# Respacing a weight load, a third band slot for the first group, and another place for table loads in a kernel's own planner

## The chip, the cores and the metric

The kernel runs on one core of one Trainium2 chip. The metric is the device time of one execution in microseconds (us); the figure for a kernel is the median of several runs.

## The reference

Two branches share the input x (2048 rows of 1024, bf16), and a gate mixes them:

```
g = sigmoid((x * gate_w).sum(-1))
a = A(x, wqkv, wo)        # attention over 8 keys at distance 0, 2, ... 14; 32 heads of 32
z = gelu(x @ w_in)        # 2048 x 3584; z1 is the first half, z2 = layernorm(second half)
b = (z1 * (w_sp @ z2 + b_sp)) @ w_out
out = g * a + (1 - g) * b
```

In A, q, k and v come from x @ wqkv. Each position has a softmax over its 8 scores per head, weights the 8 values with it, and the result is multiplied by wo.

## The kernel before, in words

The work is one long sequence of matmuls on TensorE with everything else laid beside it. In order: transposes of x and the v tiles of three head groups (`vp_tile`, L297); the projections q and k of eight groups of four heads (`qk_tile`, matmul L292, copy L295 on ScalarE); v of the other groups by a Strassen scheme (`v_quad`); the z2 half of x @ w_in (`z2_tile` with matmul L821, then `z2_quad`); the z1 half (`z1_quad`); the spatial product; the output product. All Strassen matmuls are recorded at L434.

**Bands.** The scores of a group are small matmuls of q against a band of k (L354), copied from PSUM by ScalarE (L362) into a band slot in SBUF, stored to memory (`band_d`), and loaded back as `att_L` with one row of 8 scores per position (`load_bands`, L649). A band slot can be written again only when its store has been read out. Group 0 has four such copies (`first_bands`): the first into a slot of its own, three into `band_slots`; groups 1 to 7 have three, of which two go into `band_slots`.

**Attention.** VectorE takes maxima of `att_L` (L670 to L673), ScalarE the exponential (L661), VectorE the sums, weights and att_A (L682 to L691), then the products with v (L707) and their sums (L711, L712, L716). The result is stored to `o_d`.

**Gate.** A column of each v tile (copied to `gl_s`, L305, behind the tile's copy L304) holds the gate's sum; one matmul, L404, turns it, once all sixteen are there.

**Weights for z2.** `load_wz(0)` (L800) loads the first half of them in eight parts of two DMAs each. `load_later` (L924) gives the parts to the planner, due at a start and then at equal gaps. Once all eight have landed, four VectorE steps of `wz_sums` (L576) are put in line. The z2 tiles read the weights, the z2 quads the sums too. A later call, `load_later(1, ...)` (L968), does the same for the second half.

**The planner.** From L942 on the order of every engine's instructions is set by a model that runs while the program is written. It has a clock for each of TensorE, ScalarE, VectorE, SP and the DMA engines; `take` (L233) adds a duration to a clock, not sooner than a ready time. Main work (matmuls) is written in a fixed order. Before each step `advance(t)` (L763) picks, by the clocks, which attention steps of VectorE, exponentials of ScalarE and DMAs of SP are written next. The engines then run their instructions in just that order, whatever the true times are. All these DMAs are issued by SP, one after the other. Parts of `load_wz` are "timed": each is made to wait for the last ScalarE instruction that was written before it (L271 to L277), so that it can't start early. The band loads are written only when no band store is still due (L737). A change of ScalarE's function table is counted by `table(name)` (L242).

**The z2 quads.** `chain` (L498) runs seven products. The third, Y, is added to a stored share by VectorE (`plus`, L505), and a later product writes Y again; two quads run in turns, so TensorE has three other products before it needs that sum.

Of the kernel before, what the change touches and what calls it, by code (L numbers as in the profile page):

```python
# [43 lines left out]
R_OFF = XS_OFF + 16384  # L44
# [3 lines left out]
VP = GP * C  # L48
# [5 lines left out]
def _sub_ap(t, offset_elems, dims):  # L54
    return bass.AP(tensor=t.tensor, offset=t.offset + offset_elems, ap=[list(t.ap[0])] + [list(d) for d in dims])
# [3 lines left out]
def kernel(  # L59
# [26 lines left out]
    def reg(off, n):  # L86
        return arena[:, off:off + n]
# [44 lines left out]
    band_slots = [reg(R_OFF + o, 7 * BR).bitcast(F16).rearrange("p (m k h) -> p m k h", m=7, h=HG) for o in (30208, 32196, 38848)]  # L132
    band0 = reg(R_OFF + 34184, 2 * BR).bitcast(F16).rearrange("p (m k h) -> p m k h", m=2, h=HG)
    nc.gpsimd.memset(band0[:, :, 0:W - 1, :], NEG)
    vst_slots = [reg(R_OFF + o, 2 * VR).rearrange("p (a c) -> p a c", a=2) for o in (19968, 34752, 36288, 37824)]
    vp_slots = [reg(R_OFF + o, 4 * VP).rearrange("p (i c) -> p i c", i=4) for o in (36288, 37824, 4096, 5632)]
    vq_slots = [reg(R_OFF + 39360 + 2 * VH * r, 2 * VH).bitcast(F32) for r in range(2)]
    vz_slots = [reg(R_OFF + 19968 + 2 * ZC * r, 2 * ZC).bitcast(F32) for r in range(2)]

# [63 lines left out]
    clock = dict(PE=0.0, ACT=0.0, DVE=0.0, SP=0.0, DMA=0.0)  # L203
# [29 lines left out]
    def take(engine, dur, ready=0.0):  # L233
        clock[engine] = max(clock[engine], ready) + dur
        return clock[engine]

    def pe(dur, ready=0.0):
        return take("PE", dur, ready)

    tables = ["exp"]  # L240

    def table(name):  # L242
        t = 0.0 if tables[0] == name else 1.28
        tables[0] = name
        return t

    def act(dur, ready):
        if live[0]:
            advance(ready)
        return take("ACT", dur, ready)  # L250
# [6 lines left out]
    def dma(ready, dur, f, landed=None, timed=False):  # L257
        if not live[0]:
            return f()
        item = [ready, dur, f, landed, timed]  # L260
        due.append(item)
        return item

    def issue(item):
        if item in due:
            due.remove(item)
            ready, dur, f, landed, timed = item
            sp = take("SP", 0.62, max(ready, lanes[-8]))
            end = take("DMA", 1.2 * dur, sp + 0.6) + 1.1
            lanes.append(end)  # L270
            if timed:  # L271
                settle()
                behind, at = pinned[gate_act.ins.engine], len(nc.cur_bb.bb.instructions)
            f()
            if timed:
                for i in nc.cur_bb.bb.instructions[at:]:
                    tc.add_manual_dep(i, behind, SYNC, reason="not sooner")  # L277
            if landed is not None:
                landed(end)
# [48 lines left out]
    band_at = [0]  # L328
# [7 lines left out]
    def band_blocks(g, first, step, n, pairs=None):  # L336
        qt, kt_ = qT_slots[g % 2], kT_slots[g % 2]
        if first == 0:
            st = band0
        else:  # L340
            st = band_slots[band_at[0] % (3 if g else 2)]
            band_at[0] += 1
        for item in stored.get(id(st), ()):
            issue(item)
        ready = pe(T_BAND * (0.3 if n < 3 else 1.0), band_free[0])
        lo = W - 1 if first == 0 else 0
        for m in range(n):
            e, b = divmod(first + m * step, 8) if pairs is None else (m // pairs, first + m % pairs)
            for q in range(2):
                skip = lo if q == 0 else 0  # L350
                at = P * b + QB * q
                for h in range(HG):
                    hp = slice(DH * h, DH * (h + 1))
                    nc.tensor.matmul(banks[4 + h][QB * q:QB * (q + 1), m * KW + skip:(m + 1) * KW], qt[hp, e, at:at + QB],  # L354
                                     kt_[hp, e, at - (W - 1) + skip:at + QB], start=True, stop=True,
                                     tile_position=(DH * h, QB * q), skip_group_check=True)
        band_free[0] = act(0.55 if n < 3 else 1.73, ready + 0.2) + 0.15
        if lo:
            nc.scalar.copy(st[QB:P, 0:n, 0:lo, :], _sub_ap(psum_all[QB:P, :], 4 * 512, [[KW, n], [1, lo], [512, HG]]))
        dst = st[:, 0:n, lo:KW, :]  # L360
        src = _sub_ap(psum_all, 4 * 512 + lo, [[KW, n], [1, KW - lo], [512, HG]])
        nc.scalar.copy(dst, src)  # L362
        bd = band_d[g]

        def landed(t):
            band_data[g] = max(band_data[g], t)

        stored[id(st)] = []
        for q in range(2):
            for e in range(1 if pairs is None else 2):  # L370
                k = n if pairs is None else pairs
                dst = bass.AP(tensor=bd.tensor, offset=bd.offset + (2 * first + 16 * e + q) * BS, ap=[[BR, QB], [2 * step * BS, k], [1, BR]])
                src = st[QB * q:QB * (q + 1), e * k:(e + 1) * k].rearrange("p m k h -> p m (k h)")
                stored[id(st)].append(dma(band_free[0], 0.1 * k, lambda dst=dst, src=src: sync.dma_start(dst, src), landed))

    def band_set(g, x):
        band_blocks(g, *BAND_SETS[x])
# [422 lines left out]
    def load_wz(p):  # L800
        def part(k):
            for m in range(2):
                sync.dma_start(wz[p][m][:, k:k + 1], win_v[:, k:k + 1, FH + ZC * (2 * m + p):FH + ZC * (2 * m + p + 1)])
        return [lambda k=k: part(k) for k in range(KT)]


    def wz_sums(p):
        w = wz[p]
        return sums4_steps(wzs[p], w[0][:, 0:4], w[0][:, 4:8], w[1][:, 0:4], w[1][:, 4:8])
# [66 lines left out]
    def group_tiles(g):  # L876
        if g + 1 < NG:
            tiles = [lambda t=t, c=c: qk_tile(g + 1, t, c) for t in range(2) for c in range(4)][not g:]
        else:
            tiles = [lambda a=a, m=m: z2_tile(7, a, m) for m in range(2) for a in range(2)]  # L880
        if g == 0:
            return tiles

        def band(x):
            band_set(g, x)
            if x == 2:
                bands_have[0] = g + 1
        band = [lambda x=x, f=band: f(x) for x in range(3)]
        if g + 1 < NG:
            return [tiles[0], band[0], tiles[1], band[1], tiles[2], tiles[3], band[2]] + tiles[4:]  # L890
        return [tiles[0], band[0], tiles[1], band[1], tiles[2], band[2]] + tiles[3:]

    def with_quads(g, main):
        n = NQ[g]
        if not n:
            return main
        steps = [lambda: mark(banks[5:7], ZC)]
        for _ in range(n):
            q = z2_quad(*quads.pop(0), side=1)
            steps += [lambda q=q: next(q)] * 7  # L900
        rest = main[6:]
        out, done = main[0:6], 0
        for m, t in enumerate(rest):
            out.append(t)
            upto = len(steps) * (m + 1) // len(rest)
            out += steps[done:upto]
            done = upto
        return out
# [4 lines left out]
    def behind_first(n):  # L913
        at = [0]

        def f():
            at[0] += 1
            if at[0] == 1:
                mark(banks[5:7], n)
            step()  # L920
        return f

    def play(items):
        for f in items:  # L924
            f()
            step()

    def load_later(p, at, gap):
        land = [0.0]

        def landed(t):
            land[0] += 1
            if land[0] == KT:
                fill.extend((t + LATE, 1.05, f) for f in wz_sums(p))
        for n, f in enumerate(load_wz(p)):
            dma(at + gap * n, 0.65, f, landed, True)

    def load_wqk_later(g, at):
        dma(at, 2.9, lambda: load_wqk(g, sync.dma_start))
# [13 lines left out]
    for g in range(NG):  # L953
        main = with_quads(g, group_tiles(g))
        if g in (1, 2, 3, 4):
            load_wqk_later(g + 3, clock["PE"])
        hold[0] = g == NG - 1
        play(main[0:8 - (not g)])
        if g == 2:
            for i in range(0, 8, 2):  # L960
                run(v_quad(i), v_quad(i + 1), step=behind_first(VH) if i == 0 else step)
            advance(clock["PE"] + 1.0)
            v_have[0] = NG
            next_v()
            load_later(0, clock["PE"] + 6.0, 3.0)
        play(main[8 - (not g):])

    load_later(1, clock["PE"] + 3.0, 2.0)  # L968
# [1 line left out]
    for n in range(0, len(quads), 2):  # L970
        p, i = quads[n]
        if p == 1 or quads[n + 1][0] == 1:
            t = clock["PE"]
# [398 lines left out]
```

## Time and profile before

| | us |
|---|---|
| median of 6 runs | 671.29 (668.59 to 672.04) |
| profiled execution, its own time | 672.14 |
| its span, first to last instruction | 670.4 |
| TensorE busy in the span | 658.7 |
| VectorE busy | 451.7 |
| ScalarE busy | 293.7 |
| DMA queue of SP, share of 16 engines | 60.3% |

A profile is of one execution. A row of a timeline gives start, duration, engine, source line, operation, output and inputs with their sizes, the count of merged instructions, and in square brackets how long the engine had been idle before it and what released it. A row of waits gives who waited for whom: us in total, times, longest. The granted clock is the share of full speed that TensorE was allowed. The lines that matter are shown in the prediction.

### The profile page before, as it was taken

What the parts mean: (1) busy time and instruction counts of PE and PEld (TensorE: products, weight loads), DVE (VectorE), ACT (ScalarE), POOL (GpSimd) and SP (SyncE); (2) the same over time, 40 slices, a digit from 0 to 9 for tenths busy, and PEclk for the clock granted to TensorE, in tenths of its full rate; (3) what the DMA queues carried; (4) which work ended last, traced back from release to release, by engine and by line L of the source; (5) the groups of instructions that cost most, each with busy time, mean ns of one, the idle gap of its engine ahead of it and who ended that gap; (6) DMA issues with size and microseconds to landing.
All of it is one profiled execution on the core that took longest, in us unless ns stands there. A gap on an engine that the chain in (4) does not pass through costs nothing.

```text
span 670.4 us, 10740 instructions
## 1 busy us (share of the span) xinstructions
PE 658.7 (98%) x4194; PEld 316.9 (47%) x4194; DVE 451.7 (67%) x671; ACT 293.7 (44%) x621; POOL 6.6 (1%) x15
## 2 busy tenths in 40 slices
PE   8989999999998999999999999999999999999998
PEld 4544467444444555444444444444444444444444
DVE  1520799966998999998779676797679953333301
ACT  4444676555686668789745112111122122222221
POOL 1000000000000000001100000000000000000000
PEclk9999999999997999999999999999999999999999
DMA  9988564698585132246993578559755788534100
GB/s 213 184 210 229 112 119 129 155 238 176 128 198 121 62 88 67 64 123 171 256 264 125 137 181 165 123 171 292 114 133 148 151 189 198 120 98 101 40 33 32
DMA packets 229475, 98.16 MB, mean 146 GB/s; under 512 B 177440, under 2 KB 215728, under 8 KB 229424
## 3 DMA queue, kind: packets, MB, share of 16 engines
q1 hardware_dynamic: 229136, 97.27, 60.3%
q8 instruction: 33, 0.54, 0.4%
q10 hardware_dynamic: 288, 0.20, 0.1%
q14 instruction: 18, 0.15, 0.1%
HBM read 45.10 MB, written 36.61 MB: 122 GB/s over the span
## 4 chain that ended last, share of the span: by engine, by line
PE 84%; DVE 6%; DMA 4%; SPq 4%; issue 1%; ACT 1%; DVEq 0%; ACTq 0%
PE psum_all L434 68%; PE psum_all L292 12%; SPq L195 3%; DVE arena L707 2%; PE psum_all L302 2%; DMA band_d<-arena 2%; DVE arena L711 1%; PE psum_all L354 1%; DMA att_L<-band_d 1%; SPq L190 1%; DMA arena<-in_A_x_dram 1%; DMA z_d<-arena 1%; DVE arena L712 1%; DVE arena L716 0%; PE psum_all L490 0%
## 5 line engine op out<-in xcount | busy, mean ns | idle before, releaser
L434 PE MATMUL psum_all<-arena 128*128 128x512 bf16 (+5 forms) x2425 | 498.7, 368 | 3.4 <-DVE psum_all L505 3.3
L434 PEld LDWEIGHTS <-arena 128*128 128x128 f16 (+1 forms) x2425 | 238.0, 98 | 263.0 <-issue 8.2
L292 PE MATMUL psum_all<-arena 128*128 128x512 bf16 x512 | 114.8, 379 | 0.0
L292 PEld LDWEIGHTS <-arena 128*128 128x128 bf16 x512 | 48.5, 98 | 56.2 <-issue 0.2
L707 DVE TENSOR_TENSOR arena<-arena,att_A 128x2048 f16<-128x2048 bf16 (+1 forms) x44 | 73.4, 1705 | 0.3
L295 ACT CAST arena<-psum_all 128x512 bf16<-128x512 f32 x64 | 36.9, 587 | 44.8 <-PE psum_all L292 44.7
L580 DVE TENSOR_TENSOR arena<-arena 128x1024 f16<-128x1024 f16 (+3 forms) x31 | 18.8, 608 | 46.1 <-PE psum_all L434 40.8
L452 ACT COPY psum_all<-psum_all 128x512 f32<-128x512 f32 (+1 forms) x30 | 15.8, 527 | 76.6 <-PE psum_all L434 73.0
L814 ACT ACTIVATE arena<-psum_all 128x448 bf16<-128x448 f32 x64 | 34.2, 545 | 23.1 <-DVE psum_all L505 12.9
L505 DVE TENSOR_TENSOR psum_all<-psum_all,arena 128x448 f32<-128x448 f32 (+1 forms) x58 | 37.1, 660 | 6.7 <-PE psum_all L434 4.3
L1094 ACT ACTIVATE arena<-psum_all 128x512 bf16<-128x512 f32 x56 | 31.1, 602 | 22.2 <-PE psum_all L434 13.1
L582 DVE TENSOR_TENSOR arena<-arena 128x1024 f16<-128x1024 f16 (+3 forms) x31 | 18.6, 607 | 31.6 <-PE psum_all L434 18.6
L711 DVE TENSOR_TENSOR arena<-arena 128x2048 f16<-128x2048 f16 (+1 forms) x22 | 37.2, 1704 | 0.1
L362 ACT CAST arena<-psum_all 128x1988 f16<-128x1988 f32 (+3 forms) x25 | 33.9, 1356 | 6.3 <-DMA band_d<-arena 5.1
L476 ACT COPY psum_all<-psum_all 128x512 f32<-128x512 f32 (+2 forms) x30 | 15.6, 522 | 46.2 <-PE psum_all L434 45.2
L458 ACT COPY arena<-psum_all 128x512 f32<-128x512 f32 (+1 forms) x30 | 16.2, 543 | 37.2 <-PE psum_all L434 33.1
L463 ACT COPY psum_all<-psum_all 128x512 f32<-128x512 f32 (+1 forms) x30 | 15.8, 528 | 36.4 <-PE psum_all L434 35.6
L869 ACT ACTIVATE arena<-arena 128x896 bf16<-128x896 bf16 x32 | 30.5, 961 | 0.0
L581 DVE TENSOR_TENSOR arena<-arena 128x1024 f16<-128x1024 f16 (+3 forms) x31 | 18.4, 607 | 10.4 <-PE psum_all L434 10.3
L1296 DVE TENSOR_TENSOR arena<-psum_all,arena 128x512 bf16<-128x512 f32 x8 | 5.5, 691 | 29.3 <-ACT psum_all L476 29.3
L302 PE MATMUL psum_all<-arena 128*128 128x385 bf16 x128 | 22.6, 327 | 0.0
L576 DVE TENSOR_TENSOR arena<-arena 128x512 f16<-128x512 bf16 (+3 forms) x36 | 19.4, 568 | 4.1 <-DMA arena<-in_B_w_in_dram 2.3
(95 smaller groups left out, 402.1 us busy)
## 6 DMA issues: line engine op xcount, KB each, us to landing
arena<-v_d SPq DMA_DIRECT2D x8, 960.0 KB, 7.6
z_d<-arena SPq DMA_DIRECT2D x14, 512.0 KB, 4.8
arena<-z_d SPq DMA_DIRECT2D x14, 512.0 KB, 4.2
zg_d<-arena SPq DMA_DIRECT2D x56, 128.0 KB, 2.2
arena<-zg_d SPq DMA_DIRECT2D x32, 224.0 KB, 3.2
band_d<-arena SPq DMA_DIRECT2D x28, 248.5 KB, 5.0
arena<-in_A_wqkv_dram SPq DMA_DIRECT2D x16, 256.0 KB, 4.3
o_d<-arena SPq DMA_DIRECT2D x4, 1024.0 KB, 6.7
```

The source lines that it names most:

```text
L195: inst = _orig_dmat(*a, **k)
L292: nc.tensor.matmul(ps[:], w[:, t, kt, :], xT[:, kt, 512 * c:512 * (c + 1)], start=(kt == 0), stop=(kt == KT - 1))
L295: nc.scalar.copy(dst[:, :, 256 * c:256 * (c + 1)], ps[:].rearrange("p (n e) -> p e n", e=2))
L302: nc.tensor.matmul(ps[:, 0:VP + 1], xT[:, kt, i * P:(i + 1) * P], wvp[:, kt, :], start=(kt == 0), stop=(kt == KT - 1))
L362: nc.scalar.copy(dst, src)
L434: nc.tensor.matmul(bank[:, 0:N], lhsT, rhs, start=(start and m == 0), stop=(m == n - 1), skip_group_check=True)
L505: last_add[0] = nc.vector.tensor_tensor(out[:, n], a[:, n], vs, ALU.add)
L707: lambda ws=ws, in0=in0, in1=in1: tt(p5[:, ws], in0[:, ws], in1[:, ws], ALU.mult)), False
L711: lambda a=p3[:, ws], b=p3[:, ws.start + 4:ws.stop + 4]: tt(a, a, b, ALU.add)), not n
L814: nc.scalar.activation(z2[:, i + 8 * a, ZC * c:ZC * (c + 1)], bank[:, 0:ZC], ACT.Gelu_apprx_tanh, accum_out=s1[:, 4 * n + c:4 * n + c + 1])
L869: return nc.scalar.activation(junk, src, ACT.Square, accum_out=(s2, s2h)[x][:, n:n + 1])
L1094: last_gelu[0] = nc.scalar.activation(z1s[:, f, a, :], bank[:], ACT.Gelu_apprx_tanh)
```

## The change

The gap between the parts of the first z2 weights goes from 3 to 6 of the planner's microseconds, and the first is due at 4 instead of 6 (last hunk). Group 0 takes turns over three band slots instead of two; since the third slot overlaps the second of the slots for v tiles (`vp_slots`), that one moves from offset 37824 to 16128, inside the second buffer of `v_slots_t`. `table` no longer returns a duration that the caller adds behind the ready time; it advances ScalarE's clock itself, before the caller's ready time is looked at.

```diff
-    vp_slots = [reg(R_OFF + o, 4 * VP).rearrange("p (i c) -> p i c", i=4) for o in (36288, 37824, 4096, 5632)]
+    vp_slots = [reg(R_OFF + o, 4 * VP).rearrange("p (i c) -> p i c", i=4) for o in (36288, 16128, 4096, 5632)]
...
     def table(name):
-        t = 0.0 if tables[0] == name else 1.28
+        if tables[0] != name:
+            take("ACT", 1.28)
         tables[0] = name
-        return t
+        return 0.0
...
         if first == 0:
             st = band0
         else:
-            st = band_slots[band_at[0] % (3 if g else 2)]
+            st = band_slots[band_at[0] % 3]
             band_at[0] += 1
...
             v_have[0] = NG
             next_v()
-            load_later(0, clock["PE"] + 6.0, 3.0)
+            load_later(0, clock["PE"] + 4.0, 6.0)
         play(main[8 - (not g):])
```

## The prediction

> **What bounds the kernel now.** I read the page's first two parts, then TensorE's waits, then the timeline around each wait.
>
> ```profile
> span 670.4 us, 10740 instructions
> PE 658.7 (98%) x4194; PEld 316.9 (47%) x4194; DVE 451.7 (67%) x671; ACT 293.7 (44%) x621; POOL 6.6 (1%) x15
> PEclk9999999999997999999999999999999999999999
> ```
>
> TensorE is busy for 658.7 of 670.4 us. So a change that adds and removes no matmul can win only TensorE's 11.7 us of idle time, and whatever a lowered clock stretches. One slice of the 40, the 13th (201 to 218 us), shows a lowered clock. TensorE's waits name the idle time that other engines cause:
>
> ```profile
> PE psum_all L434 <- DVE psum_all L505: 3.3, 2, 3.1
> PE psum_all L404 <- ACT gl_s L305: 2.2, 1, 2.2
> ```
>
> Start-up takes 2.4 us of the rest and the tail 2.7; both lie outside the change. These two waits are the ones that it can reach.
>
> The 2.2 us wait, in the timeline of all engines:
>
> ```profile
> 40.66 0.48 ACT L304 CAST arena<-psum_all 128x384 bf16<-128x384 f32 x1 [0.72 <-PE psum_all L302]
> 41.03 0.17 ACT L305 COPY gl_s<-psum_all 128x1 f32<-128x1 f32 x1
> 46.29 1.10 ACT L362 CAST arena<-psum_all 128x1136 f16<-128x1136 f32 x1 [5.09 <-DMA band_d<-arena]
> 48.88 0.38 PE L404 MATMUL psum_all<-ident,gl_s 128*16 128x128 f32 x2 [2.24 <-ACT gl_s L305]
> ```
>
> ScalarE stands for 5.09 us in front of L362, the fourth band copy of group 0: it reuses the first slot, whose store is still in flight. Six short copies (L304, L305) stand behind it, and the gate matmul L404 needs the last.
>
> The 3.1 us wait, by TensorE's windows (columns: stretch, its length, busy time and matmuls, granted clock, DMA share, GB/s) and then the timeline of all engines:
>
> ```profile
> 200.00:202.00 2.00, 0.00 (x0) 1.00 1.22 163
> 202.00:203.00 1.00, 0.05 (x1) 0.50 1.05 280
> 208.00:209.00 1.00, 1.00 (x4) 0.59 0.00 0
> 209.00:210.00 1.00, 1.00 (x8) 1.00 0.62 159
> ```
>
> ```profile
> 197.86 4.49 DVE L707 TENSOR_TENSOR arena<-arena,att_A 128x4096 f16<-128x4096 bf16 x2
> 202.27 0.63 DVE L505 TENSOR_TENSOR psum_all<-psum_all,arena 128x448 f32<-128x448 f32 x1
> 202.95 1.28 PE L434 MATMUL psum_all<-arena 128*128 128x448 f16 x3 [3.08 <-DVE psum_all L505]
> ```
>
> VectorE runs two attention products (L707) ahead of the first sum (L505) of the z2 quads, in the order that the program wrote, and comes to L505 late. TensorE idles 3.08 us and then runs at half clock from 202.95 to about 208.8.
>
> Why is VectorE late? Its own timeline, and SP's:
>
> ```profile
> 153.63 0.29 DVE L670 TENSOR_TENSOR att_m<-att_L 128x256 f16<-128x256 f16 x1 [7.58 <-DMA att_L<-band_d]
> 144.37 2.09 SPq L190 DMA_DIRECT2D arena<-in_B_w_in_dram  x2
> 146.55 0.59 SPq L190 DMA_DIRECT2D band_d<-arena  x1
> 147.19 2.60 SPq L190 DMA_DIRECT2D arena<-in_B_w_in_dram  x2
> 149.84 1.28 SPq L190 DMA_DIRECT2D att_L<-band_d  x2
> ```
>
> It stood 7.58 us for the scores of a group (att_L). SP issues from 126 to 151 us with hardly a gap, and seven of the eight pairs of first z2 weights (arena<-in_B_w_in_dram) stand ahead of that att_L load.
>
> **The change, part by part.**
>
> *Third band slot for group 0.* It removes L362's wait for a DMA and adds no instruction. L362 can then start when ScalarE has done L305 at 41.20, with its matmuls already done at 40.89, so about 5 us earlier. The vp tiles whose copies follow end on TensorE at 44.9; the last gl_s copy would be done by about 45.6 (0.48 + 0.17 behind it). L404 stands behind L292, which ends at 46.64, so the whole 2.24 us go. What is late next: nothing before 46.64. Where the 2.2 us could be given back: the stores of these bands do not come sooner, since SP issues eight band stores back to back from 44.97 to 50.19. The scores of group 0 thus still land at 65.5. The exponential that needs them starts at 69.9 on ScalarE, behind TensorE's work in ScalarE's order; 2.2 us sooner is 67.7, still after L673 ends at 66.8. So the attention moves with TensorE. The vp slot that has to make room moves into the second v buffer, which is loaded only after that slot's stores: bounds 0 and about 1 us, on SP beside busy TensorE; I take 0. Gain: **2.2**.
>
> *Spacing of the z2 weights.* The eight pairs took 0.82, 2.28, 1.33, 1.29, 1.13, 2.09, 2.60 and 0.85 us of SP's timeline, 12.4 us in all, 1.55 each. In the planner's time they were due at 6, 9, ... 27; they become due at 4, 10, ... 46. The att_L load fell between the seventh and the eighth (24 and 27). By 24 the new spacing has issued four (4, 10, 16, 22). Three pairs fewer ahead of it: 3 x 1.55 = 4.6 us sooner. VectorE's other waits of this stretch fall with it: 1.07 us at 136.51, for a store of o_d that stands behind the second pair (2.28), and 1.56 us at 159.30, where the weight sums (L576, four of 1.06) waited for the last pair's data. Together 4.6 + 1.07 + 1.56 = 7.2 us of VectorE's time before 202. To meet TensorE, L505 must come 3.08 us sooner (5.3 if VectorE did not share the 2.2 us above). The planner's own order can spend some of the room: one more L707 of 2.29 us in front of L505. That leaves between 7.2 - 3.08 = 4.1 us of margin and 7.2 - 5.3 - 2.3 = -0.4. I count the wait as gone, with a remainder in the sum below.
>
> What the wait is worth: 3.08 us idle, and 5.9 us at half clock, which cost 2.95: **6.0**. The Trainium skill (TensorE: Matmul & The Clock Gate, Part 1) has the clock fall after an idle window of about 3.4 us. By that rule, read as a threshold, a 3.08 us gap would cost 3.1 only, and the whole sum below be 4.8. The clock row shows 0.50 behind this gap, so I take 6.0. The 2.24 us gap at 46.6 shows no fall (1.00 in that stretch).
>
> What the move costs: five pairs pass the att_L loads of later groups on SP. The last pair is due 19 planner microseconds later, so at about 152.6 + 19 = 172. Landing takes a median 3.9 us (page, DMA issues), so 176, against L821 (z2 tiles, which read these weights) at 184.98 - 2.2 = 182.8: 7 us of cover. The sums move from 159 to about 176 and are wanted at about 194.
>
> *Table loads in the planner.* No instruction is added; the planner lets ScalarE's 1.28 us pass before the data is ready. This agrees with the first gelu's load at 185.78, which starts in the row right behind the copy that ends at 185.77 and is done at 187.06, while its matmuls end at 186.66: 0.4 us of it is in the way, not 1.28. The Trainium skill (ScalarE: Activation LUTs, What ACT_TABLE_LOAD costs) adds 1.38 us of drain to each switch. The row has no such gap; by the rule the gelu would start 1.4 us later than it did, and the planner should count 2.66, which would put L505 later again. I take the row: the planner's TensorE clock falls by some 1 us in group 7, which puts L505 a little sooner in VectorE's order. Worth 0 by itself (bounds: +0.5 and -0.5).
>
> *New lateness after 203.* In the old run the half clock let VectorE catch up: between 203 and 350 its L505 waited on TensorE 18 times for 4.3 us. That cover shrinks. The nearest row for what then happens is at 272 to 277, where four L707 in front of L505 cost TensorE 0.31 us. Bounds: 0 and four such L707 (4 x 1.16 = 4.6 us). I take 0.5.
>
> Sum: 2.2 + 6.0 - 0.5 = **7.7 us**. The profiled execution took 672.14 us; it becomes 664.4. It lies 0.85 above the median of the runs (671.29), so the prediction is **663.6**.
>
> **Rivals.**
>
> *The wait stays in part.* For: VectorE is 90 to 100% busy from 160 to 350, and the planner fills new room with attention work. Against: 7.2 us of freed time. If 1.5 to 3 us of waiting remain, with or without the half clock, or come back between 203 and 350, the gain is 3 to 6: 665 to 668.5.
>
> *The spacing does nothing for TensorE.* If att_L is held by its own stores' landing (SP waits up to 2.5 us for band_d) and not by the queue, only the band slot remains: 671.3 - 2.2 = 669.1.
>
> *Slower: the moved pairs hold SP.* Each pair waits, by construction, for the last ScalarE instruction written before it. From 154 to 178 ScalarE itself stands 3.62, 3.42 and 1.56 us for VectorE (L661). If the pairs inherit these 8.6 us and add their own 5 x 1.55 = 7.8, less the some 7 us in which SP was idle between 153 and 190, the later att_L loads come 9.4 us later. That is more than the 7.2 gained: L505 then comes 2.2 us later than before, TensorE 2.2 sooner, the wait grows by 4.4, and the time is 671.3 - 2.2 + 4.4 = 673.5. It decides once those loads come over 7.2 us later. Against: the pairs are due in step with ScalarE's order, and the exponentials come sooner too.
>
> **How the numbers follow.** Main case 0.62 (662 to 665.2), wait in part 0.20 (to 668.5), band slot alone 0.07 (669.1), slower or level 0.11 (to 675). The range 661.5 to 669.0 leaves out the last and a little below. About 0.3%, 2.0 us, can be told from no change: faster 0.86, same 0.05, slower 0.09.
>
> **What would show it.** Right: no wait of L404; L362 without a DMA wait; granted clock 1.00 from 200 to 210; the wait of L670 for att_L near 150 us down from 7.6 to some 3; TensorE's busy time down by 3 to about 655.7, its idle time by 5. Wrong: L821 waiting for in_B_w_in_dram, an att_L wait after 160 us above 3 us, a new clock fall, or TensorE waiting for L505 between 203 and 280.

## The result, and the profile after

| | before | changed |
|---|---|---|
| median, us | 670.53 (36 runs, 667.52 to 674.14) | 665.45 (17 runs, 664.45 to 670.12) |
| ratio to before, 95% interval | | 0.9934 [0.9918, 0.9951] |
| profiled execution, its own time, us | 672.14 | 670.12 |

The ratio of the means is 0.9934, which is 4.4 us [3.3, 5.5] of 670.5; the two medians differ by 5.1. The forecast was 663.6, a gain of 7.7 us: the direction holds, the size does not, and the rival "the wait stays in part" (665 to 668.5) describes what came. The execution that was profiled is the slowest of the changed kernel's 17, as the one of before had been one of the slow ones, so the two pages must not be subtracted from each other. The page of the changed kernel (all its line numbers past 242 are one higher than before: L506 is L505, L708 is L707):

```profile
span 668.0 us, 10747 instructions
PE 659.0 (99%) x4194; PEld 317.1 (47%) x4194; DVE 452.2 (68%) x671; ACT 294.5 (44%) x621; POOL 6.2 (1%) x15
PEclk9999999999998999999999999999999999999999
```

The lowered clock is still there, in the same slice, the 13th (0.8, before 0.7). TensorE's waits, all that are over 1 us:

```profile
PE psum_all L435 <- DVE psum_all L506: 3.3, 1, 3.3
PE psum_all L318 <- DVE arena L313: 1.2, 1, 1.2
```

The gate matmul (L405) is gone from the list; the first sum (L506) is not. The timeline around the gate:

```profile
41.25 0.17 ACT L306 COPY gl_s<-psum_all 128x1 f32<-128x1 f32 x1
41.30 1.12 ACT L363 CAST arena<-psum_all 128x1136 f16<-128x1136 f32 x1
...
45.54 0.17 ACT L306 COPY gl_s<-psum_all 128x1 f32<-128x1 f32 x1
...
46.79 0.39 PE L405 MATMUL psum_all<-ident,gl_s 128*16 128x128 f32 x2
```

L363 follows the copy before it at once; the last gl_s is done at 45.7 (the prediction said 45.6), and L405 has no bracket. So the band slot did what its working said. The other place, TensorE's windows and then VectorE's and TensorE's rows:

```profile
198.00:200.00 2.00, 0.00 (x0) 0.97 0.98 247
200.00:202.00 2.00, 1.00 (x3) 0.50 0.79 149
206.00:208.00 2.00, 2.00 (x11) 0.82 0.90 239
```

```profile
149.40 0.29 DVE L671 TENSOR_TENSOR att_m<-att_L 128x256 f16<-128x256 f16 x1 [6.47 <-DMA att_L<-band_d]
...
200.32 0.63 DVE L506 TENSOR_TENSOR psum_all<-psum_all,arena 128x448 f32<-128x448 f32 x1
...
201.00 11.28 PE L435 MATMUL psum_all<-arena 128*128 128x448 f16 x44 [3.27 <-DVE psum_all L506]
```

The wait for the scores, which was to fall from 7.58 to about 3, is 6.47; TensorE stands 3.27 us instead of 3.08, and the half clock follows (0.50 until 206). SP's rows show the reason's first half:

```profile
136.06 5.37 SPq L190 DMA_DIRECT2D arena<-in_A_wqkv_dram  x2
141.53 2.37 SPq L190 DMA_DIRECT2D arena<-in_B_w_in_dram  x2
143.95 1.28 SPq L190 DMA_DIRECT2D att_L<-band_d  x2
```

Only four pairs of w_in now stand ahead of att_L, three fewer, as foretold. But the load of q and k weights in front of it holds SP for 5.37 us where before it took 2.50, and from the issue of att_L to VectorE's first use of it there are 5.45 us (143.95 to 149.40), before 3.79 (149.84 to 153.63).

### The profile page after: what moved, and what is told of

It reads as the page before. It is cut to its first block, busy times and chain, and to the rows that moved or that the text cites. A ratio compares the mean times of both kernels' runs of the same rounds, so it can differ in the third digit from the quotient of the medians.

```text
span 668.0 us, 10747 instructions
## 1 busy us (share of the span) xinstructions
PE 659.0 (99%) x4194; PEld 317.1 (47%) x4194; DVE 452.2 (68%) x671; ACT 294.5 (44%) x621; POOL 6.2 (1%) x15
## 4 chain that ended last, share of the span: by engine, by line
PE 88%; DVE 5%; DMA 3%; ACT 1%; issue 1%; SPq 0%; DVEq 0%
PE psum_all L435 73%; PE psum_all L293 11%; PE psum_all L303 3%; DVE arena L708 2%; DMA att_L<-band_d 2%; DMA band_d<-arena 1%; PE psum_all L355 1%; DVE arena L712 1%; DMA arena<-in_A_x_dram 1%; DVE arena L713 1%; ACT arena L815 0%; PE psum_all L491 0%; DVE arena L717 0%; ACT arena L363 0%; DVE arena L577 0%
## 5 line engine op out<-in xcount | busy, mean ns | idle before, releaser
L293 PE MATMUL psum_all<-arena 128*128 128x512 bf16 x512 | 114.8, 379 | 0.0
L293 PEld LDWEIGHTS <-arena 128*128 128x128 bf16 x512 | 48.4, 98 | 56.2 <-issue 0.2
L708 DVE TENSOR_TENSOR arena<-arena,att_A 128x2048 f16<-128x2048 bf16 (+1 forms) x44 | 73.3, 1704 | 0.3
L506 DVE TENSOR_TENSOR psum_all<-psum_all,arena 128x448 f32<-128x448 f32 (+1 forms) x58 | 37.5, 661 | 6.5 <-PE psum_all L435 4.5
L712 DVE TENSOR_TENSOR arena<-arena 128x2048 f16<-128x2048 f16 (+1 forms) x22 | 37.2, 1704 | 0.1
L363 ACT CAST arena<-psum_all 128x1988 f16<-128x1988 f32 (+3 forms) x25 | 33.9, 1356 | 1.2 <-PE psum_all L355 0.4
L671 DVE TENSOR_TENSOR att_m<-att_L 128x256 f16<-128x256 f16 x8 | 2.3, 288 | 29.6 <-DMA att_L<-band_d 29.6
```

Source lines behind the costliest of these rows:

```text
L293: nc.tensor.matmul(ps[:], w[:, t, kt, :], xT[:, kt, 512 * c:512 * (c + 1)], start=(kt == 0), stop=(kt == KT - 1))
L506: last_add[0] = nc.vector.tensor_tensor(out[:, n], a[:, n], vs, ALU.add)
L708: lambda ws=ws, in0=in0, in1=in1: tt(p5[:, ws], in0[:, ws], in1[:, ws], ALU.mult)), False
L712: lambda a=p3[:, ws], b=p3[:, ws.start + 4:ws.stop + 4]: tt(a, a, b, ALU.add)), not n
```

## The experiments

All kernels, each against the kernel before on the same chip (e1 to e4 on one, e5 to e8 on a second, f1 to f4 on a third). "Clock" counts executions by their mean granted TensorE clock: 0.999 or 1.00, or 0.997, or 0.992 to 0.995. In the profiles the first means no fall of the clock, the second one stretch of 3.4 us at half clock (it costs up to 1.7 us), and 0.994 or 0.995 two such stretches (up to 3.4 us); no execution at 0.992 was profiled. "Gate" and "sum" are TensorE's waits in us at the gate and at the first sum in the one profiled execution.

| kernel | median us (runs) | ratio [95%] | clock | gate | sum |
|---|---|---|---|---|---|
| before, on two chips | (60) | 1 | 23 / 28 / 9 | 2.24 | 3.08 |
| changed, first result and e4_all | (23) | | 19 / 3 / 1 | 0 | 3.27, 1.09 |
| e1_slot | 667.68 (8) | 0.9960 [0.9941, 0.9979] | 4 / 4 / 0 | 0 | 2.45 |
| e2_space | 669.99 (12) | 0.9994 [0.9973, 1.0014] | 4 / 6 / 2 | 1.63 | 1.35 |
| e3_table | 671.47 (12) | 1.0009 [0.9988, 1.0031] | 5 / 5 / 2 | 1.67 | 2.89 |
| e4_all | 666.18 (6) | 0.9938 [0.9920, 0.9955] | 5 / 1 / 0 | 0 | 1.09 |
| e5_slot_space | 667.03 (12) | 0.9961 [0.9942, 0.9979] | 6 / 6 / 0 | 0 | 2.72 |
| e6_warm | 671.51 (12) | 1.0041 [1.0016, 1.0066] | 3 / 4 / 5 | 1.54 | 2.07 (of an added matmul) |
| e7_lag | 666.86 (12) | 0.9954 [0.9935, 0.9973] | 12 / 0 / 0 | 0 | 0.24 |
| e8_wz24 | 667.20 (12) | 0.9962 [0.9942, 0.9981] | 8 / 3 / 1 | 0 | 0.81 |
| f1_before_less | 667.91 (12) | 0.9970 [0.9950, 0.9990] | 5 / 7 / 0 | 2.81 | 0 |
| f2_all_less | 665.24 (6) | 0.9927 [0.9902, 0.9952] | 6 / 0 / 0 | 0 | 0.82 |
| f3_before_profile | 671.51 (1) | | 0 / 1 / 0 | 2.91 | 3.12 |
| f4_space_profile | 669.13 (1) | | 0 / 1 / 0 | 2.50 | 1.36 |

**Each part alone.** The change has three parts, so the first question is which of them carries the gain. First the band slot:

```diff
-    vp_slots = [... for o in (36288, 37824, 4096, 5632)]
+    vp_slots = [... for o in (36288, 16128, 4096, 5632)]
...
-            st = band_slots[band_at[0] % (3 if g else 2)]
+            st = band_slots[band_at[0] % 3]
```

> The band slot alone (both of its lines), nothing else. All theories: the gate matmul no longer waits (2.2 us before), so the time falls by 2.2 us, 0.9967 of before, if the later part of the kernel shifts along. Theory A (the attention moves with TensorE): the wait of TensorE for the first sum of the z2 quads stays at about 3.1 us, with the clock at half behind it. Rival: the scores land no sooner in absolute time, so that wait grows by up to 2.2 us and the time stays within 0.1% of before.

It gains 2.7 us [1.4, 4.0]. VectorE's wait for att_L is 8.01 (before 7.58): the attention moved with TensorE, as said. Then the spacing:

```diff
-            load_later(0, clock["PE"] + 6.0, 3.0)
+            load_later(0, clock["PE"] + 4.0, 6.0)
```

> The spacing alone. Theory A (fewer weight loads ahead of the scores on SP): the 7.6 us wait of VectorE for att_L falls by about 4, the wait for the first sum goes, the time falls by 5 to 6 us (0.991 to 0.993). Theory B (DMA traffic, not SP's list, sets when the scores land): the att_L wait falls by 1 to 2 us only, the first sum stays about 2 to 3 us late, and what is won is the half clock in those executions in which the gap stays short enough: 2 to 4 us (0.994 to 0.997), with a spread of some 4 us between executions.

No gain that can be measured, 0.4 us [-0.9, 1.8], though its profile shows every step of the mechanism:

```profile
147.36 0.29 DVE L670 TENSOR_TENSOR att_m<-att_L 128x256 f16<-128x256 f16 x1 [3.00 <-DMA att_L<-band_d]
...
200.53 9.81 PE L434 MATMUL psum_all<-arena 128*128 128x448 f16 x51 [1.35 <-DVE psum_all L505]
```

The 7.6 us for att_L became 3.00. That this is just the predicted figure is luck: two errors cancel, as the account of the spacing below shows. TensorE's wait only fell to 1.35. Third, the table loads:

```diff
-        t = 0.0 if tables[0] == name else 1.28
+        if tables[0] != name:
+            take("ACT", 1.28)
         tables[0] = name
-        return t
+        return 0.0
```

> The planner's table loads alone. Theory A: within 0.1% of before; its order differs only around the last group. Rival: by moving the planner's TensorE clock back by 1 us it changes how much attention work stands ahead of the first sum of the z2 quads, and so the wait there by 1 us or more; the sign is then read from the wait.

Alone it is worth nothing (1.0009 [0.9988, 1.0031]), as predicted. With these went the changed kernel once more:

> The changed kernel as it is, once more, for a second profile and its share of executions with a lowered clock. Theory A: like its first profile, 3.3 us of wait and half clock behind it, only in some executions; 0.993 of before. Theory B: most executions have a granted clock of 1.00 and a span some 4 us below those with a lowered clock; a profile of such a one shows a wait for the first sum below 3 us, not zero.

It repeats the first result (0.9938), and its profile, of an execution at clock 1.00, is the one to read instead of the first:

```profile
148.87 0.29 DVE L671 TENSOR_TENSOR att_m<-att_L 128x256 f16<-128x256 f16 x1 [5.71 <-DMA att_L<-band_d]
...
196.19 2.28 DVE L712 TENSOR_TENSOR arena<-arena 128x4096 f16<-128x4096 f16 x1
198.39 0.63 DVE L506 TENSOR_TENSOR psum_all<-psum_all,arena 128x448 f32<-128x448 f32 x1
...
199.07 10.75 PE L435 MATMUL psum_all<-arena 128*128 128x448 f16 x56 [1.09 <-DVE psum_all L506]
```

**Slot and spacing without the table part**, to see what the table part does in company:

> Band slot and spacing, without the planner's table loads. Its order lets L711 and L712 of one half group stand ahead of the first sum (1.22 us more than in the changed kernel). Theory A (table worth 0): 0.9935 to 0.995 like the changed kernel. Theory B (each microsecond of lateness at the first sum decides on the half clock): a wait of about 1 us more than in the changed kernel, the half clock in more of the executions, 1 to 3 us above it (0.995 to 0.998).

```profile
196.18 2.28 DVE L711 TENSOR_TENSOR arena<-arena 128x4096 f16<-128x4096 f16 x1
198.50 1.22 DVE L712 TENSOR_TENSOR arena<-arena 128x2048 f16<-128x2048 f16 x1
199.64 0.62 DVE L505 TENSOR_TENSOR psum_all<-psum_all,arena 128x448 f32<-128x448 f32 x1
...
200.32 14.91 PE L434 MATMUL psum_all<-arena 128*128 128x448 f16 x78 [2.72 <-DVE psum_all L505]
```

From 174.6 us to the large sum at 196.2 the two VectorE timelines agree within 0.01 us (the rows of e4_all stand above). Without the table part one more sum (L712, 1.22 us) stands ahead of the first L505, which comes 1.25 us later; TensorE's wait is 2.72, not 1.09. So the part that costs and gains nothing alone decides here which of two instructions goes first. In the time it is 0.9961 against 0.9938, on two chips; these intervals overlap, so a gain of 1.5 us from it is not shown.

**The idle gap filled.** The theory to be tried: the half clock is worth as much as the gap. In the kernel before, 24 matmuls of 64 columns that add into unused columns of the banks were put ahead of the product that waits:

```diff
             count[0] += 1
+            if n == 0 and count[0] == 8:
+                for k in range(24):
+                    nc.tensor.matmul(banks[k % 8][:, ZC:512], xT[:, 4, 0:P], xT[:, 4, 0:512 - ZC], start=False, ...)
```

> The kernel before, with 24 additional matmuls of 64 columns, into PSUM columns that nothing reads, right before the product that waits for the first sum: TensorE stays busy for some 1.5 us of the 3.1 us wait, and the wait's end stays. Theory B (an idle gap of about 3 us halves the clock for some 6 us, which costs 3 us by itself): granted clock 1.00 from 200 to 210, time 2 to 3 us below before (0.9955 to 0.997), although the first sum comes as late as it did. Rival (the clock is not tied to this gap): half clock as before, time the same or up to 0.3 us more.

```profile
202.08 0.28 PE L989 MATMUL psum_all<-arena 128*128 128x64 bf16 x4 [2.07 <-DVE psum_all L505]
202.81 1.17 PE L989 MATMUL psum_all<-arena 128*128 128x64 bf16 x19 [0.46 <-DVE psum_all L505]
```

The added matmuls themselves waited for the sum (they share its banks), and ran behind the gap instead of in it. The kernel is 2.7 us [1.1, 4.4] slower, of which the added matmuls take 1.6, and the clock falls in 9 of 12 executions. So the test failed: it can't say what an idle gap that is truly filled would do to the clock.

**The planner told that VectorE is late**, in the changed kernel, so that it writes less attention ahead of the first sum:

```diff
             step()
+            if n == 0 and count[0] == 1:
+                clock["DVE"] += 2.5
             count[0] += 1
```

> The changed kernel, and the planner's VectorE clock is set 2.5 us later once, at the second product of the first z2 quads, so that L711 (2.28 us) is written behind the first sum and not ahead of it. If the lateness of VectorE at that sum is all that is left there: its wait falls by up to 2.3 us to 0 to 1 us, no execution shows a lowered clock, the time is 1 to 2 us below the changed kernel (0.991 to 0.9925 of before). Rival (the work is only put off): TensorE waits for a later sum of the same quads by as much, and the time stays at 0.993 to 0.994.

```profile
197.62 10.75 PE L435 MATMUL psum_all<-arena 128*128 128x448 f16 x56 [0.24 <-DVE psum_all L506]
209.36 2.81 PE L435 MATMUL psum_all<-arena 128*128 128x448 f16 x14 [0.99 <-DVE psum_all L506]
```

The first wait is gone (0.24) and the clock falls in none of 12 executions, yet the kernel is not faster than the changed one: waits for L506 now come five times, 2.7 us in all, none above 1.0. VectorE's lateness was put off, not removed: the expectation's rival came true, as far as one profile tells.

**The weights later still**, so that no pair stands ahead of the first att_L load:

```diff
-            load_later(0, clock["PE"] + 4.0, 6.0)
+            load_later(0, clock["PE"] + 24.0, 3.0)
```

> The changed kernel with the first z2 weights due at 24, 27, ... 45 of the planner instead of 4, 10, ... 46: no pair of them is written ahead of the att_L load. Theory A (the pairs ahead on SP hold the scores back): the wait of VectorE for att_L near 149 us falls from about 6 us to 1 or 2, the first sum comes in time, 0.990 to 0.992. Theory B (the other traffic there, the loads of the next q and k weights, the v load and the o_d store, holds it): the wait stays above 4 us and the time at 0.993 to 0.995.

```profile
143.94 0.29 DVE L671 TENSOR_TENSOR att_m<-att_L 128x256 f16<-128x256 f16 x1 [1.37 <-DMA att_L<-band_d]
...
160.03 0.29 DVE L671 TENSOR_TENSOR att_m<-att_L 128x256 f16<-128x256 f16 x1 [3.92 <-DMA att_L<-band_d]
```

The first wait for scores falls to 1.37, as theory A said, but the time stays at 0.9962 and not at 0.990 to 0.992. The next group's wait grows to 3.92 (1.36 in e4_all): five pairs now stand on SP between the two att_L loads, two in e4_all, so it seems that the pairs hold the next load back instead. This is the slower rival's mechanism in small; it gives back a part and does not make the kernel slower than before.

**What the first-sum wait is worth.** In both kernels VectorE's products of the second half of group 3 were left out (two of 2.25 us, so attention is incomplete), to bring the first sum about 4.5 us forward:

```diff
-    lambda ws=ws, in0=in0, in1=in1: tt(p5[:, ws], in0[:, ws], in1[:, ws], ALU.mult)
+    lambda ws=ws, in0=in0, in1=in1, out=(g, e) == (3, 1): None if out else tt(p5[:, ws], in0[:, ws], in1[:, ws], ALU.mult)
```

> The kernel before, with two products of the attention left out (L707 of the second half of group 3, 2 x 2.29 us of VectorE; that half group's output is wrong), everything else in the same order: VectorE comes 4.5 us sooner to the first sum of the z2 quads. It measures what that wait costs in all, idle time and half clock. As predicted (3.1 idle and 3.0 clock): 6 us less than before, 0.991. By the executions seen so far (mean clock loss 1.6 us, a wait of 2 to 3 us): 3.5 to 4.5 us, 0.9935 to 0.995, and a granted clock of 1.00 in all executions.

> The changed kernel, with the same two products left out (that half group's output is wrong). If VectorE's lateness is all that is left in this stretch: 1 to 2 us below the changed kernel (0.991 to 0.9925 of before), clock 1.00 throughout, and the difference to the other kernel of this call that leaves them out is the band slot's 1.5 to 2.2 us alone. Rival (something else of the change is worth more): the difference between the two is above 3 us.

TensorE's waits in f1:

```profile
PE psum_all L404 <- ACT gl_s L305: 2.8, 1, 2.8
...
PE psum_all L434 <- DVE psum_all L505: 0.5, 2, 0.3
```

In f1 the first-sum wait is gone (the 0.5 are two later sums), and the mean of its 12 executions is 667.98, that of the kernel before on the same chip 670.13. So the whole wait, gap and clock together, is worth 2.1 us on the mean (by the ratio 2.0 [0.7, 3.4]), not the 6.0 of the prediction. f2 is 2.6 us below f1 (mean 665.34). Neither has a first-sum wait of over 0.9 us, so what separates them should be the band slot: 2.6 here, 2.7 in e1. And f2 (0.9927) is not the expected 1 to 2 us below the changed kernel (0.9934): their intervals overlap almost wholly, so what the changed kernel still waits at the first sum costs little.

**Where the clock falls.** A second profile each of the kernel before and of the spacing alone, on the chip of f1:

> The kernel before, unchanged, for a second profile. If the first profile was an unusually slow execution: gate wait near 1.6 us instead of 2.2, a wait for the first sum of 2 to 3 us, half clock for about 3.4 us or not at all instead of 5.9. If it was a usual one: 2.2, 3.1 and 5.9 us again.

> The spacing alone, for a second profile. Its first profile (span 664.7 us, att_L wait 3.0, first sum 1.4 us late, no half clock) was the fastest of 12 executions, whose median lies on that of before. If the landing of att_L varies from execution to execution: an att_L wait of 5 to 7 us and a first sum 2.5 us late or more. If the att_L wait is again near 3 us, the lost gain must sit elsewhere (another wait of TensorE).

TensorE's windows in f3, around the gate and then around the first sum:

```profile
46.00:48.00 2.00, 0.35 (x2) 1.00 0.61 139
...
50.00:52.00 2.00, 2.00 (x7) 0.63 0.52 122
52.00:54.00 2.00, 2.00 (x6) 0.52 0.85 188
...
202.00:204.00 2.00, 0.12 (x1) 1.00 1.17 167
204.00:206.00 2.00, 0.76 (x5) 1.00 0.78 195
206.00:208.00 2.00, 2.00 (x12) 1.00 0.82 98
```

Here the clock falls behind the gate's gap of 2.91 us, and not behind the first sum's of 3.12, in the very kernel whose first profile showed the opposite. In f4 it fell behind a gate gap of 2.50 us (from 49 to 53 us). Otherwise f4 repeats the first profile of the spacing almost to the hundredth (3.00 and 1.35 there):

```profile
149.93 0.29 DVE L670 TENSOR_TENSOR att_m<-att_L 128x256 f16<-128x256 f16 x1 [2.97 <-DMA att_L<-band_d]
```

TensorE then waits 1.36 us for the first sum. So the landing of att_L is not what made the median of the spacing alone so poor; by its expectation the lost gain must sit elsewhere, and in this profile the gate shows 2.50 us and a fall.

The counts of the table agree. A fall of the clock came in 37 of 60 executions where both gaps are long (before), in 15 of 24 where the gate's is the only one over 1.4 us (e2, f1), in 10 of 20 where only the first sum's is (e1, e5), and in 4 of 30 where the profile shows neither above 0.9 (e7 and f2 none, e8 four); the changed kernel, with 1.09 in the one profile and 3.27 in the other, has 4 of 23. So closing one of the two gaps leaves most of the falls, which is likely a part of why the spacing alone gains nothing measurable.

## Why the prediction was right in direction and too large

**Band slot, 2.2: right, a little small.** L363 waits for no DMA, L405 for nothing. It is worth 2.7 us by e1 and 2.6 by f2 against f1. The first profile showed one gate wait of 2.24; others have 1.54 to 2.91, and behind some of them the clock falls (f3, f4), which the prediction had excluded by the one profile that it had. f1 against f2 shows that share: 1.2 us of granted clock lost on the mean in f1, none in f2.

**Spacing, the step "three pairs fewer, 7.2 us of VectorE's time": nearly right alone, wrong in company.** The chain can be counted on VectorE from the batch of eight v copies (L626, at 115.77 us before) to the first L505: the length of that stretch, the waits in it, and the large and small sums (L711, L712) written into it.

| kernel | length us | waits us | L711 / L712 | TensorE's first-sum wait |
|---|---|---|---|---|
| before | 86.50 | 11.88 | 6 / 6 | 3.08 |
| e1_slot | 86.32 | 11.73 | 6 / 6 | 2.45 |
| e2_space | 84.71 | 6.78 | 7 / 7 | 1.35 |
| e5_slot_space | 86.22 | 8.12 | 7 / 7 | 2.72 |
| e4_all | 84.45 | 7.77 | 7 / 6 | 1.09 |
| changed, first profile | 86.63 | 9.86 | 7 / 6 | 3.27 |

The rows close. In e2 the waits fall by 5.1, the planner writes one L711 (2.28) and one L712 (1.22) more into the stretch, 1.6 are left, and TensorE's wait falls by 1.7. In e4 the waits fall by 4.1, one L711 more, 1.8 left, TensorE's wait falls by 2.0. In the first profile of the changed kernel the waits fall by only 2.0, the L711 takes 2.3, nothing is left, and the wait is as long as before. So two terms were mis-sized: the freed time, 2.0 to 5.1 us for 7.2, and the spending of it, for which the prediction had a bound (one instruction of 2.29) and then counted the wait as gone.

The 7.2 can be taken apart. Counted from the same batch, att_L was issued 3.8 to 5.7 us sooner than before (4.6 was predicted, so this step was right). The 1.07 us for o_d were counted twice: that wait lies ahead of the wait for att_L, so without it VectorE only comes earlier to scores that are not there yet. (In e2 the load was issued 5.7 us sooner and this 1.07 was added to the wait, which is how it came to 3.00.) The 1.56 at the weight sums (its own row names a band store, those of e1, e3 and f3 the weights) did go, but the next wait for att_L took it up in part: it was 0.98 before, and 2.81 in e2, 1.54 in the first profile of the changed kernel, 1.36 in e4.

With slot and spacing together att_L also took longer from its issue to VectorE's first use of it, 4.95 to 5.50 us (e5, first profile, e4) for 3.79 before and 3.85 in e2, and SP was held longer ahead of it: the load of q and k weights took 5.37, 5.86 and 3.97 us (first profile, e5, e4), and 2.50, 1.33, 1.73 and 2.46 in before, e1, e2 and f4. Why was not settled. The DMA share in that stretch (135 to 140 us) is 1.0 to 1.1 with and without; and f2, which has all parts and other work on VectorE, took 1.98 and waited 3.30 for att_L, so it hangs on the timing and not on the parts alone. In e8 the load took 4.12 with no pair of z2 weights ahead of it, so these pairs alone are not the cause.

**"What the wait is worth: 6.0": the step that failed most.** The sum was made against one execution, at clock 0.994, with two stretches, 6.8 us, at half clock at the first sum; only 9 of 60 executions of that kernel are of this kind. It lay only 0.85 us above the median of the six runs, which made it look typical. The median over the 60, 669.96, lies between those of the executions without a fall and with one: 668.80 and 670.42; with two it is 672.67. On the mean the wait is worth 2.1 (f1): without it the clock still falls in 7 of 12 executions, at the gate as far as f3 and f4 show, so the clock's share of it was 0.4 us (1.6 lost on the mean before on that chip, 1.2 in f1) and not 2.95. The 4.4 us of the result are about 3.4 between the medians at clock 1.00 (668.80 and 665.44), and 1.2 for the falls (on the mean 1.6 us of them before, 0.4 after).

The rule of the Trainium skill (TensorE: Matmul & The Clock Gate, Part 1) that the prediction weighed there, an idle window of about 3.4 us that runs free of the kernel, fits in one respect: the same gap falls in one execution and not in the next. As a threshold it doesn't fit: the clock fell behind gaps of 2.50, 2.89, 2.91, 3.08 and 3.27 us, and stayed at 1.00 behind 2.24, 2.45, 2.72, 2.81 and 3.12 (e6, where one added matmul breaks the gap, is not counted). The sum by the rule, 4.8, is nearer to the 4.4 measured than the 7.7 by the row, but not for the rule's reason: that is luck. That the wait is worth even less than its gap of 3.1 us is not explained; the interval of f1 reaches to 3.4. Both profiles that show a gap of 3.1 are of executions slower than the median (672.14 and 671.51), so in most executions it may be shorter; no run shows that.

**Table loads, 0: right alone.** In company they take one 1.22 us sum from in front of the first L506 (e5 against e4), the "little sooner" of the text.

**New lateness after 203, 0.5.** e4_all has a second wait for L506 of about 1.0 us; the size was right within half a microsecond, and e7 shows that this is where VectorE's lateness goes when it is taken from the first sum.

**The rivals.** "The wait stays in part" was the case (0.20). "Band slot alone" is near: spacing and table add some 1.7 to its 2.7, where 5.5 was predicted (6.0 less 0.5); the intervals of e1 and e4 overlap, so even this is likely and not shown, and the spacing without the table adds nothing measurable (e5 against e1, on two chips). The slower one did not come: the later waits for att_L are 1.54 and 1.15 us in the first profile of the changed kernel, and L822 waits for no weights. Of the other signs, TensorE's busy time tells little between profiles (659.0, and 657.2 in e4_all): the first 36 us alone differ by 1 us between them.

That the direction held is owed in good part to the band slot: the 6.0 of the spacing, most of the sum of 7.7, failed.

No version that computes the whole result beat the changed kernel.

## What to carry to other kernels

A stall of some 3 us in one profile is better priced at no more than its gap (here 2.1 us on the mean for 3.1); add the clock behind it only as a share of executions, ask whether another gap would make the clock fall anyway, and ask first which kind of execution the profile is. Taking away a wait that ends in front of a longer wait for something else frees no time: don't add the two. In an order that a planner writes, freed time on a busy engine is spent by the planner: count what it will put into the room before counting the wait as gone. The part that was harmless alone, the table loads, set the order of two sums once the others were in, so such a part is to be tried with the others too.

## What was not expected of the hardware

Gaps of the same size give no, one or two stretches of 3.4 us at half clock (f3 none behind 3.12 us; e3 one behind 2.89; before two behind 3.08). What decides between them stays open.

One thing that looks like hardware is not. In the profiles on two of the chips (e5 to e8 and f1 to f4) TensorE seems to stand 12 or 13 times for 0.16 us ahead of L292 (L293) with nothing that the profile names. But in each of these traces 58 matmuls are missing, 24 of the 512 of L292 among them: the page of f1, like f3's, has 4136 matmuls (PE) to 4194 weight loads (PEld), where the one of before has 4194 of both. First before, then f1:

```profile
126.82 0.65 PE L354 MATMUL psum_all<-arena 32*64 32x71 bf16 x56
127.40 3.63 PE L292 MATMUL psum_all<-arena 128*128 128x512 bf16 x16
130.96 0.65 PE L354 MATMUL psum_all<-arena 32*64 32x71 bf16 x56
...
127.32 0.65 PE L354 MATMUL psum_all<-arena 32*64 32x71 bf16 x56
128.12 3.40 PE L292 MATMUL psum_all<-arena 128*128 128x512 bf16 x15 [0.16 <-issue]
131.46 0.65 PE L354 MATMUL psum_all<-arena 32*64 32x71 bf16 x56
```

From one L354 to the next it is 4.14 us in both, with 16 matmuls and with 15: the piece of 0.16 us is a matmul whose record is missing, and no time is lost there.
